# First transforms from half-height matrices into a two-bank buffer, fewer banks for the other tiles, and tap 0 added on GpSimd

## The chip, the cores and the metric

The kernel runs on one core of one Trainium2 chip. The metric is the device time of one execution in microseconds (us), as the median of several runs. TensorE (PE in the profile) multiplies matrices into PSUM, which has eight banks of 128 x 512 floats; VectorE (DVE) and ScalarE (ACT) read PSUM and SBUF; GpSimd (POOL) works on SBUF alone; SyncE (SP) issues most DMAs. All data are float32.

## The reference, cut to what matters

Four layers in a row update x (2048 positions, 512 channels): A, B, A, B. Each layer is a long causal convolution per channel.

```python
def A(q, k, v, shift_k, ssm_k, ssm_D):
    k_shift = sum of 4 shifted copies of k, each times shift_k     # short causal convolution
    kv = k_shift * v
    y  = irfft(rfft(kv, 4096) * rfft(ssm_k, 4096))[:2048]          # per channel
    return q * (y + kv * ssm_D)

def B(u, ...):
    K[d, l] = 2 * Re(sum over 128 modes n of C[d, n] * exp(A[d, n] * dt[d] * l))
    y = irfft(rfft(u, 4096) * rfft(K, 4096))[:2048]                # per channel
    return y + u * D_skip

x = q
x = x + A(layernorm(x), k, v, ...)
x = x + B(layernorm(x), ...)
x = x + A(layernorm(x), k, v, ...)      # same k, v: the same convolution result as in the first A
x = x + B(layernorm(x), ...)            # same K
```

`ssm_D` and `D_skip` are direct terms: the same as adding them to element 0 (tap 0) of the convolution kernels before the transform.

## The kernel before, in words

**The transform.** An FFT of 4096 points is done as two matrix stages with a transpose between them. The sequence is laid out on 128 partitions as two halves of 64 rows (a = 0, 1), 16 positions deep, and the channels are taken in 4 quarters (q) of 4 groups (g) of 32. The first stage (`fwd_rows`, L171, tile `pf`) multiplies each group by the matrix `wz[:, a, :]`, in which only the 64 rows of half a hold numbers and the other 64 hold zeros: a matmul over all 128 rows, two per step, with a step of 16 channels, so that both halves of a step fill one bank. VectorE then transposes 32 x 32 blocks from `pf` into `z` (L195, or L193 where a step is 32 channels wide). Where the tag `f1` exists, which is only in the second half of the program, a step is 32 channels: two matmuls of 512 columns over 64 rows each, with the matrix `w1`, stand side by side on the upper and the lower rows of the array and write two banks. The second stage (`f2_chunk`, L200, tile `pu`) does 8 chunks of 4 matmuls for a quarter.

**Spectra.** `spectrum_quarter` makes the spectrum of a convolution kernel: it loads a group `kk` by DMA (from the input `ssmk_in` for A, from `kdram` for B), transforms it with `fwd_group`, and adds the direct term with a third matmul of one row and 16 columns per step (L187, from `dr`, "tap 0"). After the eight chunks, ScalarE copies each `pu` to `pc` (L245) and a DMA writes it to `spec`.

**The convolution.** `convolution` takes for each of 32 steps a chunk `pu` of the data's spectrum, reads it with ScalarE (`sw`, L277, L278) and VectorE (`vv`, L279), multiplies by the loaded spectrum `kab` on GpSimd (L281, L282), transforms back in two stages (`pi` L291, `po` L312) and hands groups to `finish`.

**Two streams at once.** `diagonal` computes A: the four spectra of A, the short convolution and product (`gated`, L604 to L619, stored to `kv_d`), and the convolution of A. `stream` computes the kernel K of B (`taps`): `mags` (matmul L467 into `pm`, exponential on ScalarE, L469), `angles` (L479, L483, L484, tile `pa`), `waves` (sines on ScalarE, L492 to L494), `products` (L505 to L509 on GpSimd and VectorE) and `contract` (L520, tile `pk`), for 16 groups of 4 pieces; exponentials are made for two groups at a time, twelve in a run, because sines and exponentials need different tables on ScalarE. After every four groups it makes one quarter of B's spectrum. `run_steps` takes one step of `stream` and two of `diagonal` in turn; a list scheduler then fixes the order on each engine, which is in-order on the chip.

**PSUM in this first half.** Three banks with the tag `c1` hold `pf`, `pu`, `pi` and `po` of A and the first forward transforms of B's data; two banks `pm` hold the exponents and also `pf` and `pu` of B's spectrum; two hold `pa`, one holds `pk`. In the second half the banks are divided anew (four `c1`, two buffers of two banks `f1`).

**Afterwards.** `gated_update` loads the result of A (`yaq` from `ya_d`), updates x and its statistics (L715 to L724), then `conv_b(0)` convolves with K, a second `gated_update` uses the same A, and `conv_b(1)` writes the output. The first quarter of `conv_b(0)`'s forward transforms (`steps_b`, q = 0) is placed before the banks are divided anew.

Of the kernel before, what the change touches and what calls it, by code (L numbers as in the profile page):

```python
# [9 lines left out]
F32 = mybir.dt.float32  # L10
# [89 lines left out]
def kernel(ctx: ExitStack, tc: tile.TileContext, out, x_in, kv_in, ssmk_in, ssmd_in,  # L100
                           la_in, ai_in, cr_in, ci_in, ldt_in, ldtb_in, dsk_in,
                           w1_in, w2_in, mm_in, w4_in, minus_in, tt_in, tg1_in, tg2_in, dbg=None):
    nc = tc.nc
    V, S, G, T = nc.vector, nc.scalar, nc.gpsimd, nc.tensor
# [30 lines left out]
    wz = cpool.tile([128, 2, 128], F32, name="wz")  # L135
# [7 lines left out]
    psum, w1, swapped = {}, [], [None]  # L143

    def bank(name, tag="c1"):
        pool, bufs = psum[tag]
# [13 lines left out]
    def fwd_rows(src, pf, j, step, rows, full):  # L160
        for a in (1, 0):
            half = slice(0, 128) if full else slice(64 * a, 64 * a + 64)
            w = wz[:, a, :] if full else w1[0][half, :]
            rhs = src(half, j, step)[:, rows, :]
            o = pf[:, a].rearrange("p x t r -> p t x r")[:, rows]
            if len(rhs.shape) == 4:
                o = o.rearrange("p t (i x) r -> p t i x r", i=rhs.shape[2])
                rhs = rhs.rearrange("p t i (x r) -> p t i x r", r=2)
            else:
                rhs = rhs.rearrange("p t (x r) -> p t x r", r=2)  # L170
            yield T.matmul(o, w, rhs, start=True, stop=True)  # L171

    def fwd_group(src, z, c0, n, step, tap0=None, first=None, tag="c1", full=True, early=None):
        for j in range(0, n, step):
            rest = slice(0, 16)
            if early is not None:
                pf, rest = early, slice(8, 16)
            elif step == 32:
                pf = wide_bank()
            else:  # L180
                both = bank("pf", tag).rearrange("p (x n r) -> p x r n", n=32, r=2)
                pf = both.rearrange("p x r (a t) -> p a x t r", a=2)
            for i in fwd_rows(src, pf, j, step, rest, full):
                if first is not None:
                    after(i, first)
            if tap0 is not None:
                T.matmul(pf[:, 0, :, 0, :], wz[0:1, 0, :],  # L187
                         tap0[:, j:j + step].rearrange("p (x r) -> p x r", r=2), start=False, stop=True,
                         skip_group_check=True)
            zr = z[:, (c0 + j) // 2:(c0 + j + step) // 2].rearrange("p x k r -> p x r k")  # L190
            if step == 32:
                for r in range(2):
                    V.transpose(zr[:, :, r], pf[..., r].rearrange("p a x t -> p x a t"))  # L193
            else:
                V.transpose(zr, both)  # L195
# [28 lines left out]
    def spectrum_quarter(which, q, src, pool, zlast, zb, tag):  # L224
        z = pool.tile([128, 64, 32, 2], F32, name="zk", tag="z", bufs=zb)
        dr = pool.tile([1, 128], F32, name="dr", tag="dr", bufs=1)
        nc.sync.dma_start(dr, (ssmd_in, dsk_in)[which][:, 128 * q:128 * q + 128])
        for g in range(4):
            kk = pool.tile([128, 512], F32, name="kk", tag="kk", bufs=3 - which)
            nc.sync.dma_start(kk, src[4 * q + g])  # L230
            if which == 0:
                kv = kk.rearrange("p (t c) -> p t c", c=32)
                view = lambda ps_, j, n: kv[ps_, :, j:j + n]
            else:
                kv = kk.rearrange("p (i t c) -> p t i c", i=4, c=8)
                view = lambda ps_, j, n: kv[ps_, :, j // 8:(j + n) // 8, :]
            fwd_group(view, z, 32 * g, 32, 16, dr[:, 32 * g:32 * g + 32],
                      zlast[-zb] if len(zlast) >= zb else None, tag)
            yield
        for c in range(NCH):  # L240
            pu, ins = f2_chunk(z, c, None, tag)
# [182 lines left out]
    pctx = ExitStack()  # L424
    pp = pctx.enter_context(tc.tile_pool(name="ps", bufs=1, space=PSUM, reuse_waits="tile"))
    NPA = 2
    NPM = 2
    psum["c1"] = (pp, 7 - NPA - NPM)
    psum["pm"] = (pp, NPM)

    for tag, bufs in (("c1", 7 - NPA - NPM), ("pa", NPA), ("pk", 1)):
        pp.tile([128, 512], F32, name=tag, tag=tag, bufs=bufs)
    wk = sbuf(gctx, "wk")
    kp = sbuf(gctx, "spec_k")
    NT = 3
# [154 lines left out]
    with ExitStack() as actx:  # L590
# [42 lines left out]
        def steps_a(q):  # L633
# [7 lines left out]
            def fwd(g):  # L641
                if g == 0:
                    z[0] = ap.tile([128, 64, 32, 2], F32, name="zu", tag="z", bufs=ZA)
                u = us[g]
                fwd_group(lambda ps_, j, n: u[ps_, :, j:j + n], z[0], 32 * g, 32, 16, None, zlast[4 + q - ZA])
                if g < 3:
                    load(g + 1)
            turns = [lambda g=g: fwd(g) for g in range(4)]
# [46 lines left out]
    nc.sync.dma_start(w1[0], w1_in)  # L695
# [67 lines left out]
    def steps_b(rnd, q):  # L763
# [152 lines left out]
```

## Time and profile before

| what | value |
|---|---|
| median of the three runs | 803.81 us (801.69 to 804.71) |
| the profiled execution's own time | 802.01 us |
| its span, from the first to the last instruction | 800.2 us |
| mean granted TensorE clock | 0.862 |
| PE, DVE, ACT, POOL busy | 676.5, 604.8, 479.2, 531.9 us |

An engine's busy time is the sum of its instructions' spans; the ends of matmuls are modelled. One row for a float32 matmul stands twice in the profile's counts, since the chip runs it as two passes. PEclk is the share of the full TensorE clock that was granted. A DMA's time to landing runs from its issue.

### The profile page before, as it was taken

The numbers are of one execution on the slowest core, as the hardware profiler recorded it, in microseconds if no ns is written. First come the engines' busy times: TensorE is split into PE (matmuls) and PEld (weight loads), VectorE is DVE, ScalarE is ACT, GpSimd is POOL, SyncE is SP. The second block draws the span as 40 slices with busy tenths as digits, with TensorE's granted clock in tenths as the row PEclk, the third lists the DMA queues.
The fourth block names the chain that finished last, engine by engine and source line by source line (L and its number), as shares of the span: only waits on it lengthen the run. The fifth ranks groups of instructions, "written<-read, shape, count | busy, mean of one in ns | idle before, by whom it ended". The sixth has DMA issues, their size and how long they took to land.

```text
span 800.2 us, 14659 instructions
## 1 busy us (share of the span) xinstructions
PE 676.5 (85%) x5192; PEld 475.6 (59%) x5192; DVE 604.8 (76%) x939; ACT 479.2 (60%) x881; POOL 531.9 (66%) x464
## 2 busy tenths in 40 slices
PE   3779988999989999999899867889789840898996
PEld 2555755667667766757666444666557720476673
DVE  7767856989996958756849699625568989878775
ACT  4144443535478884785884687628746625878572
POOL 4966744967868975777964678206666836288783
PEclk9686765869999999999999755699989975999998
DMA  9586254557378463664541891238968541078792
GB/s 329 195 263 249 94 174 151 187 171 253 130 222 231 131 184 97 192 187 153 125 119 54 268 313 42 76 115 206 238 169 197 147 106 53 1 182 220 200 247 99
DMA packets 89614, 135.49 MB, mean 169 GB/s; under 512 B 8509, under 2 KB 37701, under 8 KB 89029
## 3 DMA queue, kind: packets, MB, share of 16 engines
q1 hardware_dynamic: 88644, 132.13, 56.8%
q0 software_dynamic: 896, 2.43, 1.0%
q8 instruction: 41, 0.67, 0.4%
q14 instruction: 33, 0.26, 0.1%
HBM read 98.87 MB, written 35.65 MB: 168 GB/s over the span
## 4 chain that ended last, share of the span: by engine, by line
PE 27%; DVE 14%; ACT 4%; DMA 4%; issue 3%; POOL 2%; SPq 1%; DVEq 0%; POOLq 0%; ACTq 0%
PE pu L200 8%; PE pf L171 6%; PE pi L291 5%; PE po L312 5%; DVE x L722 3%; DVE ut L715 2%; DMA kab<-spec 2%; POOL sw L281 1%; DMA yaq<-ya_d 1%; DVE w L306 1%; PE pk L520 1%; DVE vv L279 1%; POOL vv L282 1%; DVE tt L506 1%; DVE st L822 1%
## 5 line engine op out<-in xcount | busy, mean ns | idle before, releaser
L281 POOL TENSOR_TENSOR sw<-sw,kab 128x512 f32<-128x512 f32 x96 | 125.4, 1313 | 76.5 <-ACT sw L278 65.5
L505 POOL TENSOR_TENSOR xy<-tt,m 128x512 f32<-128x512 f32 x64 | 89.7, 1402 | 62.7 <-ACT tt L494 54.6
L200 PEld LDWEIGHTS pu<-zu,w 128*128 128x128 f32 x768 | 94.6, 191 | 51.1 <-DVE vv L279 18.4
L200 PE MATMUL pu<-zu,w 128*128 128x128 f32 x768 | 108.4, 283 | 12.2 <-DVE vv L279 11.8
L171 PE MATMUL pf<-kk,wz 128*128 128x256 f32 x256 | 96.2, 512 | 24.7 <-DMA kk<-ssmk_in 15.9
L279 DVE TENSOR_TENSOR vv<-pu,kab 128x512 f32<-128x512 f32 x96 | 64.7, 679 | 64.6 <-ACT sw L278 32.0
L282 POOL TENSOR_TENSOR vv<-vv,sw 128x512 f32<-128x512 f32 x76 | 100.1, 1320 | 14.8 <-DVE vv L279 12.0
L291 PE MATMUL pi<-vv,mm 128*128 128x128 f32 x768 | 106.9, 284 | 3.4 <-DVE vv L279 2.8
L291 PEld LDWEIGHTS pi<-vv,mm 128*128 128x128 f32 x768 | 95.3, 195 | 15.9 <-issue 9.4
L277 ACT ACTIVATE sw<-pu 64x512 f32<-64x512 f32 x96 | 57.1, 595 | 63.0 <-PE pu L200 52.1
L200 PE MATMUL pu<-zk,w 128*128 128x128 f32 x512 | 80.4, 313 | 5.5 <-DVE zk L195 3.6
L492 ACT ACTIVATE tt<-pa 128x512 f32<-128x512 f32 x64 | 38.5, 601 | 75.4 <-PE pa L484 64.1
L200 PEld LDWEIGHTS pu<-zk,w 128*128 128x128 f32 x512 | 74.8, 223 | 14.4 <-DVE zk L195 4.1
L171 PEld LDWEIGHTS pf<-kk,wz 128*128 128x128 f32 x256 | 57.8, 247 | 42.8 <-issue 16.0
L245 ACT COPY pc<-pu 128x512 f32<-128x512 f32 x64 | 37.5, 592 | 63.1 <-PE pu L200 45.7
L469 ACT ACTIVATE m<-pm 128x512 f32<-128x512 f32 x96 | 54.2, 598 | 31.5 <-PE pm L467 30.6
L506 DVE TENSOR_TENSOR tt<-tt,m 128x512 f32<-128x512 f32 x64 | 71.6, 1118 | 0.4
L507 DVE SCALAR_TENSOR_TENSOR xy<-tt,m 128x256 f32<-128x256 f32 x64 | 51.1, 798 | 24.0 <-ACT tt L493 20.2
L195 DVE STREAM_TRANSPOSE zk<-pf 128x512 f32<-128x512 f32 x64 | 44.5, 703 | 28.0 <-PE pf L187 27.8
L312 PE MATMUL po<-w,w 128*64 128x512 f32 x192 | 56.1, 671 | 7.8 <-DVE w L306 6.7
L509 POOL TENSOR_TENSOR xy<-tt,m 128x256 f32<-128x256 f32 x64 | 60.9, 951 | 0.0
L520 PE MATMUL pk<-xy,tt 128*32 128x64 f32 x2048 | 53.7, 244 | 5.8 <-POOL xy L509 3.1
(141 smaller groups left out, 1310.3 us busy)
## 6 DMA issues: line engine op xcount, KB each, us to landing
kab<-spec SPq DMA_DIRECT2D x188, 256.0 KB, 4.0
spec<-pc SPq DMA_DIRECT2D x64, 256.0 KB, 2.4
kvt<-kv_in SPq DMA_DIRECT2D x16, 624.0 KB, 6.5
yaq<-ya_d SPq DMA_DIRECT2D x8, 1024.0 KB, 5.5
kk<-ssmk_in SPq DMA_DIRECT2D x16, 256.0 KB, 5.1
kv_d<-u SPq DMA_DIRECT2D x16, 256.0 KB
kdram<-ks SPq DMA_DIRECT2D x64, 64.0 KB, 2.4
kk<-kdram SPq DMA_DIRECT2D x16, 256.0 KB, 2.6
```

The lines of the kernel that those rows point to most:

```text
L171: yield T.matmul(o, w, rhs, start=True, stop=True)
L200: ins = T.matmul(pu[:, i, :], w2[:, c * CK + i, :], z[:, :, c * CK + i, :], start=True, stop=True)
L277: S.mul(sw[0:64], pu[64:128], -1.0)
L279: V.tensor_mul(vv, pu, kabs[s][:, 0])
L281: (V if last else G).tensor_mul(sw, sw, kabs[s][:, 1])
L282: (V if last or s % add_dve == add_dve - 1 else G).tensor_add(vv, vv, sw)
L291: i1s[t] = T.matmul(pi[:, i, :], mm[:, c * CK + i, :], vvs[t][:, i, :], start=True, stop=True)
L312: ins = T.matmul(po[64 * a:64 * a + 64], w4, ws[g][:, :, 16 * a:16 * a + 16, :].rearrange("p x t r -> p t x r"), start=True, stop=True, ti ...
L505: G.tensor_mul(xy[:, :, :, 32:64], tt[:, :, :, 1:33], m1[:, :, 32:64][:, None].to_broadcast([128, 2, 8, 32]))
L506: (G if (4 * gi + k) % E2P == E2P - 1 else V).tensor_mul(e2, e2, m2[:, None].to_broadcast([128, 2, 8, 32]))
L509: (V if (4 * gi + k) % XLP == XLP - 1 else G).tensor_mul(xy[:, 0, :, 0:32], tt[:, 0, :, 0:32], m1[:, :, 0:32])
L520: T.matmul(pk[32 * i4:32 * i4 + 32, 2 * k + i, :], e2[:, r, 4 * i + i4, :], xy[:, r, 4 * i + i4, :], start=r == 0, stop=r == 1, tile_posit ...
```

## The change

What it does:

- All first transforms but those of the first group of `conv_b(1)` use a step of 32 channels with `wz[half, a, :]`, 64 rows each, into a buffer of two banks; the separate matrix `w1` and its DMA go.
- In the first half of the program, PSUM is divided anew: `c1` two banks (three before), `pm` one (two before), `f1` one buffer of two banks (new), `pa` two and `pk` one as before. All `pf` of the first half are now in `f1`; `pu` of B's spectrum stays in `pm`.
- Tap 0 is no longer a matmul. GpSimd adds `dr` to row 0 of the loaded `kk` (1 x 32 elements) before the group's transform.

```diff
     def fwd_rows(src, pf, j, step, rows, full):
         for a in (1, 0):
             half = slice(0, 128) if full else slice(64 * a, 64 * a + 64)
-            w = wz[:, a, :] if full else w1[0][half, :]
+            w = wz[half, a, :]
...
-    def fwd_group(src, z, c0, n, step, tap0=None, first=None, tag="c1", full=True, early=None):
+    def fwd_group(src, z, c0, n, step, first=None, tag="c1", full=False, early=None):
...
-            if tap0 is not None:
-                T.matmul(pf[:, 0, :, 0, :], wz[0:1, 0, :],
-                         tap0[:, j:j + step].rearrange("p (x r) -> p x r", r=2), start=False, stop=True,
-                         skip_group_check=True)
...
     # spectrum_quarter
+            d = dr[:, 32 * g:32 * g + 32]
...
-            fwd_group(view, z, 32 * g, 32, 16, dr[:, 32 * g:32 * g + 32],
-                      zlast[-zb] if len(zlast) >= zb else None, tag)
+                d = d.rearrange("p (i c) -> p i c", c=8)
+
+            G.tensor_add(kv[0:1, 0], kv[0:1, 0], d)
+            fwd_group(view, z, 32 * g, 32, 32, zlast[-zb] if len(zlast) >= zb else None, tag)
...
-    NPM = 2
-    psum["c1"] = (pp, 7 - NPA - NPM)
+    NPM = 1
+    psum["c1"] = (pp, 2)
     psum["pm"] = (pp, NPM)
+    psum["f1"] = (pp, 1)
...
     # steps_a
-                fwd_group(lambda ps_, j, n: u[ps_, :, j:j + n], z[0], 32 * g, 32, 16, None, zlast[4 + q - ZA])
+                fwd_group(lambda ps_, j, n: u[ps_, :, j:j + n], z[0], 32 * g, 32, 32, zlast[4 + q - ZA], full=False)
...
-    w1.append(xp.tile([128, 128], F32, name="w1"))
-    nc.sync.dma_start(w1[0], w1_in)
...
     # steps_b
-                fwd_group(src(c), z[0], 16 * c, 32, 32 if "f1" in psum else 16,
-                          full="f1" not in psum or q == 0 and c < 2 * EF, early=early.get(c))
+                fwd_group(src(c), z[0], 16 * c, 32, 32, full=rnd == 1 and q == 0 and c < 2 * EF,
+                          early=early.get(c))
```

More of the change, by code (lines that the diff above doesn't have):

```diff
@@ L141 @@
     var, rs, nm, nb = [cpool.tile([128, 16], F32, name=n) for n in ("var", "rs", "nm", "nb")]
-    psum, w1, swapped = {}, [], [None]
+    psum, swapped = {}, [None]
     def bank(name, tag="c1"):
@@ L426 @@
     NPA = 2
-    NPM = 2
-    psum["c1"] = (pp, 7 - NPA - NPM)
+    NPM = 1
+    psum["c1"] = (pp, 2)
     psum["pm"] = (pp, NPM)
-    for tag, bufs in (("c1", 7 - NPA - NPM), ("pa", NPA), ("pk", 1)):
-        pp.tile([128, 512], F32, name=tag, tag=tag, bufs=bufs)
+    psum["f1"] = (pp, 1)
+    for tag, bufs, shape in (("c1", 2, [128, 512]), ("f1", 1, [128, 2, 512]), ("pa", NPA, [128, 512]), ("pk", 1, [128, 512])):
+        pp.tile(shape, F32, name=tag, tag=tag, bufs=bufs)
     wk = sbuf(gctx, "wk")
```

## The prediction

> **What bounds the kernel now.** I read the busy table of the page first, then the busy time by stretches, then the groups of instructions, then the waits, and last the chain that ended last where no engine is full.
>
> ```profile
> span 800.2 us, 14659 instructions
> 60.00:140.00 80.00, 73.09 (x453) 48.39 (x454) 54.41 (x77) 33.64 (x57) 46.64 (x37) 0.61 0.50 167
> 140.00:240.00 100.00, 91.93 (x866) 66.29 (x864) 93.48 (x136) 51.63 (x91) 78.97 (x64) 0.87 0.60 192
> 240.00:380.00 140.00, 136.62 (x1288) 100.83 (x1288) 98.71 (x139) 104.16 (x181) 105.87 (x95) 0.99 0.60 168
> 380.00:440.00 60.00, 55.39 (x547) 37.14 (x547) 44.58 (x57) 42.80 (x75) 40.09 (x34) 1.00 0.36 100
> 440.00:500.00 60.00, 43.28 (x400) 28.64 (x399) 53.56 (x85) 46.17 (x92) 45.09 (x34) 0.64 0.68 208
> 500.00:540.00 40.00, 33.46 (x246) 26.24 (x245) 17.85 (x40) 18.07 (x39) 5.05 (x10) 0.81 0.31 94
> ACT tt L492 <- PE pa L484: 60.6, 25, 8.9
> ACT m L469 <- PE pm L467: 28.9, 16, 5.6
> ```
>
> The stretches give, after their length, the busy time of PE, of its weight loads, of DVE, ACT and POOL, then the granted clock and the DMA load. The change touches only what lies before 540. From 60 to 440 PE is busy 357.0 of 380 us: 91% from 60 to 140, at a clock of 0.61, and 98% from 240 to 380 at 0.99. The last two rows (the waits of that stretch: total, times, longest) say the same from the other side: ScalarE sits behind PE. Only from 140 to 240 is another engine as full (DVE, 93.5 of 100). From 440 to 500 DVE has most, with the update of x; from 500 to 540 nothing is full, and a chain of dependent steps sets the time.
>
> **What the change takes from PE.** Here are the groups of instructions (busy us, mean ns), then the first transforms alone (PE's busy time and count by stretch) and tap 0 alone, then pieces of PE's timeline (start, length).
>
> ```profile
> L171 PE MATMUL pf<-kk,wz 128*128 128x256 f32 x256 | 96.2, 512 | 24.7 <-DMA kk<-ssmk_in 15.9 <-DVE zk L195 5.5 <-DMA kk<-kdram 2.1
> L195 DVE STREAM_TRANSPOSE zk<-pf 128x512 f32<-128x512 f32 x64 | 44.5, 703 | 28.0 <-PE pf L187 27.8
> L193 DVE STREAM_TRANSPOSE zu<-pf 128x512 f32<-128x512 f32 x56 | 35.8, 686 | 13.7 <-PE pf L171 13.5
> L467 PE MATMUL pm<-tg,rw 64*128 64x512 f32 x96 | 46.6, 556 | 13.6 <-ACT m L469 8.9 <-DVE rw L460 4.8
> L469 ACT ACTIVATE m<-pm 128x512 f32<-128x512 f32 x96 | 54.2, 598 | 31.5 <-PE pm L467 30.6
> L245 ACT COPY pc<-pu 128x512 f32<-128x512 f32 x64 | 37.5, 592 | 63.1 <-PE pu L200 45.7 <-DMA spec<-pc 17.2
> L263 POOL COPY kab<-kab 1x128 f32<-1x128 f32 x12 | 4.7, 392 | 4.0 <-DMA kab<-spec 3.5
> ```
> ```profile
> 60.00:140.00 80.00, 28.22 (x60) 15.97 (x60) 0.61 0.50 167
> 140.00:240.00 100.00, 30.81 (x96) 20.25 (x96) 0.87 0.60 192
> 240.00:380.00 140.00, 33.16 (x124) 21.59 (x124) 0.99 0.60 168
> 380.00:440.00 60.00, 9.97 (x36) 6.18 (x36) 1.00 0.36 100
> ```
> ```profile
> 60.00:140.00 80.00, 8.64 (x30) 7.05 (x30) 0.61 0.50 167
> 140.00:240.00 100.00, 7.10 (x32) 5.50 (x32) 0.87 0.60 192
> 240.00:380.00 140.00, 3.12 (x16) 2.34 (x16) 0.99 0.60 168
> 380.00:440.00 60.00, 3.12 (x16) 2.34 (x16) 1.00 0.36 100
> ```
> ```profile
> 21.85 1.13 PE L171 MATMUL pf<-kk,wz 128*128 128x256 f32 x4
> 22.91 0.39 PE L187 MATMUL pf<-dr,wz 1*128 1x16 f32 x2
> 23.23 1.13 PE L171 MATMUL pf<-kk,wz 128*128 128x256 f32 x4
> ...
> 602.24 1.13 PE L171 MATMUL pf<-u,w 64*128 64x512 f32 x4
> 603.30 1.16 PE L200 MATMUL pu<-zu,w 128*128 128x128 f32 x8
> ```
>
> A step of 16 channels stands as four records and takes 1.06 us at full clock (21.85 to 22.91); tap 0 behind it takes 0.32 (to 23.23). A group of 32 channels is two steps, so 2.12 us, and 2.76 with tap 0. The new form is in the trace already, in the second half: the two matmuls of a group over half the rows run side by side and take 1.06 us (602.24 to 603.30) for all 32 channels.
>
> By stretch: 60 records are 7.5 groups. From 60 to 140 the old form holds PE for 28.2 + 8.6 = 36.9 us; the new one 7.5 x 1.06 / 0.61 = 13.0, so 24 us go. From 140 to 240 (12 groups): 37.9 less 12 x 1.06 / 0.87 = 14.6, so 23. From 240 to 380 (15.5 groups): 36.3 less 16.4, so 20. From 380 to 440 (4.5 groups): 13.1 less 4.8, so 8. Together 75 of PE's 357 us.
>
> **What of that can become time.** PE would hold 49, 69, 117 and 47 us of 80, 100, 140 and 60, and another engine decides. From 60 to 140 that is DVE with 54.4; from 140 to 240 DVE with 93.5, so nothing is to be had there; from 240 to 380 POOL with 105.9 and ACT with 104.2; from 380 to 440 DVE with 44.6. None of them gets to work without gaps. I let the fullest be busy 85% of the time (an estimate between the 68 to 76% that they hold now in three of the stretches and the 93% of DVE in the fourth): 64, 100, 125 and 52 us, which saves 16, 0, 15 and 8, or 39 us. That is the upper end. The lower end is nothing, if the missing banks give it all back. I take half, 20 us, for this reason: three banks of `c1` become two, but the `pf` that used them leave, so `pu`, `pi`, `po` lose little; `pm` loses much more.
>
> **What the lost bank of `pm` costs.** Now PE fills one bank while ScalarE reads the other, and twelve exponentials in a run can follow each other at 0.60 us (L469). With one bank each waits for its matmul: 0.60 + 0.56 (L467) is 1.16 us, at least. That is 0.56 x 96 = 54 us more of latency over 8 runs. Where PE and ScalarE have other work between, and from 60 to 440 both have, it is hidden: the order that the scheduler built puts `pu`, `pi` or `pf` between most of these matmuls. One run has no such cover, that of the last two groups of taps, behind the end of A; it is 12 x 0.56 = 7 us longer. It lies where DVE is full with the update of x, and I count nothing for it, 7 at most. The chunks of B's spectrum have the same single bank, and there the last quarter counts, next.
>
> **GpSimd's adds.** 32 adds of one row: the nearest row is the copy of one row, 0.39 us (L263), so 12.5 us over a POOL that is busy 271.6 of 380; nothing at best, where POOL is idle. Each add waits for its `kk` at the head of POOL's queue, and products and steps of `gated` stand behind it; PE waited 15.9 us for `kk` from the input, 13 of them before its first matmul, and 2.1 for `kk` from `kdram` (row of L171), so the loads come early enough elsewhere and I count nothing before the last quarter. DVE's transposes stay as many, and as long: two per group of 0.69 (L193, reading two banks with a stride) against 0.70 (L195). The buffer `f1` is single, so the next group's matmuls wait for both: a group takes 1.06 + 1.37 = 2.4 us at least, against 2.76 on PE before; other matmuls fit in between.
>
> **From 440 on.** No engine's relief counts here but what lies on the chain that ended last:
>
> ```profile
> 445.86 0.54 SPq L695
> ...
> 499.18 1.71 PE pf L171 x4
> ...
> 501.43 2.00 PE pf L171 x4
> ...
> 505.83 2.01 PE pf L171 x4
> ...
> 508.27 1.06 PE pf L171 x4
> ...
> 519.93 2.57 DMA kk<-kdram
> ...
> 528.17 3.64 PE pu L200 x32
> 532.47 2.07 PE pu L200 x16
> 535.18 2.95 PE pu L200 x24
> ```
>
> The issue of the load of `w1` (0.54) goes. The four steps at 499 to 509, 6.8 us, become two groups of about 1.06 / 0.64 = 1.7, that is 3.3, but the second waits for the first's transposes (1.4): 2 us are saved. Then the last quarter of B's spectrum: its last `kk` lands at 522.5; the add puts 0.4 us before the transform, and at most 1.3 if POOL has a product before it. The eight chunks run from 528.17 to 537.1 (the last row holds 16 of their records and 8 of `conv_b(0)`, so 535.18 + 2/3 of 2.95): 9 us, with two banks. With one bank each chunk is matmuls (3.64 / 4 = 0.91), copy (0.59) and two hand-overs of about 0.2 (estimate): 1.9, so 15 us, 6 more. The four groups of `conv_b(0)` now fit between chunks, where PE waits anyway; without that cover they would cost 4 x 1.06. Sum of this part: -0.5 - 2 + 0.4 + 6 = +4 us; bounds -2 (chunks limited by their DMAs as now) and +13 (with the 7 and 1.3).
>
> **The sum.** 802.0 (the profiled execution) - 20 + 4 = 786. The median of the runs shown is 1.8 us above that execution, so 788 against 803.8.
>
> **The rivals.** (1) The banks do not matter: then all 39 us come, and the end takes its lower bound: 802 - 39 - 2 = 761, 763 beside the median. For it: PE waits little for banks now (8.9 us for `m` in the row of L467). Against it: ScalarE's table order and POOL's products come in bursts.
>
> (2) Slower: the one bank of `pm` becomes the pace of the taps. Place: the eight runs of exponentials, behind which no sine may start, and the 32 chunks of B's spectrum, each 0.6 us longer or more. Price: 54 + 32 x 0.7 = 76 us if none is hidden. It decides from the point where more than 20 of these 76 lie on the path besides the 6 that I count; with half of it there, 38, the time is 802 - 20 - 2 + 38 = 818, or 820 beside the median; with 32, 814. For it: already 28.9 us of ScalarE's waits are for `pm` with two banks. Against it: only one run in eight stands without other work around it.
>
> (3) The clock falls. PE has the clock of 0.99 only where it is busy 98%; at 91% (60 to 140) it has 0.61. If from 240 to 440, busy 192.0, less 28, it fell to the 0.81 of 500 to 540, PE would need 164 / 0.81 = 202 of those 200 us: 2 us more than now. With half of the 16 from 60 to 140, and the end as forecast, that is 802 + 2 - 8 + 4 = 800, or 802 beside the median; at 0.61 the 164 would be 269, far slower. The Trainium skill has such a rule in "TensorE: Matmul & The Clock Gate", Part 1, on a second failure mode: where a kernel cycles through PSUM banks and TensorE is idle for moments between groups of matmuls, the clock gate swings between half and full. By it, fewer banks would lower the clock. This trace bears it out only in part: 0.61 stands in a stretch in which PE was 91% busy.
>
> (4) The change does not do what it says: DVE, slowed by POOL beside it, bounds all of 60 to 440, and the 75 us of PE turn into idle time: 802 + 4, 808 beside the median.
>
> **How the numbers follow.** Chances: forecast 0.47 (own range 778 to 798), rival 1 0.16, rival 2 0.22, rival 3 0.07, rival 4 0.08. The likeliest is 788. The range goes from rival 1 at 763 to rival 2 with 32 of its us on the path, 814, about the middle of rival 2, so 0.11 to 0.15 stay outside. About 0.5%, 4 us, is what a measurement of this kernel can tell from no change. Faster by more than that (below 799.8): nearly all of the forecast (0.45) and rival 1 (0.16), so 0.61. Within it: 0.02 of the forecast, 0.04 of rival 3, 0.04 of rival 4: 0.10. Slower: rival 2 (0.22), 0.03 of rival 3 and 0.04 of rival 4: 0.29.
>
> **What the profile after would show.** Right: the groups `pf<-kk` with 64x512 and half the records, about 1.06 us start to start at full clock; no L187; PE's share from 240 to the end of A well under 98%, with DVE, ACT and POOL denser; the end of A (the loads of `yaq`) 15 to 25 us earlier; the last chunks of `pc` 1.9 us apart. Rival 2 would show `pm` waiting for `m`, and ScalarE's waits for `pm` far over 28.9 us; rival 3 a PEclk well under 1 from 240 to 440; rival 4 PE idle and the end of A where it is now. The forecast is wrong if the end of A does not move, or if the stretch from there to the second half grows by over 13 us.

## The result and the profile after

The changed kernel takes 849.97 us (median of four runs, 847.71 to 853.22) beside 802.75 us for the kernel before on the same chip: a ratio of 1.0635, 95% interval 1.0559 to 1.071. The profiled execution took 847.71 us, its span is 845.6. The change is slower by 6%, where 788 us were forecast. Some executions of a kernel are over 1.5% slower than its fastest; the ratios, here and below, leave these out and can differ a little from the quotients of the medians, which are of all.

The page's head and the same stretches as before come first: after the stretch's length, the busy time of PE, of its weight loads, of DVE, ACT and POOL, then the granted clock and the DMA load.

```profile
span 845.6 us, 14085 instructions
60.00:140.00 80.00, 62.13 (x482) 41.43 (x481) 69.00 (x88) 36.14 (x63) 65.90 (x56) 0.78 0.70 231
140.00:240.00 100.00, 69.52 (x592) 41.20 (x595) 71.00 (x110) 43.77 (x74) 54.74 (x51) 0.64 0.47 149
240.00:380.00 140.00, 113.93 (x1128) 75.29 (x1120) 94.81 (x128) 95.55 (x163) 97.11 (x89) 0.90 0.49 136
380.00:440.00 60.00, 53.76 (x465) 33.93 (x464) 45.04 (x55) 39.84 (x68) 39.78 (x37) 0.90 0.50 142
440.00:500.00 60.00, 48.98 (x453) 28.19 (x452) 36.19 (x48) 38.94 (x67) 32.37 (x29) 0.78 0.46 141
500.00:540.00 40.00, 23.19 (x183) 13.75 (x183) 37.77 (x67) 33.80 (x72) 26.76 (x20) 0.58 0.46 145
```

From 60 to 440 PE is busy 299.3 us, not 357.0, and no engine takes its place: over the same 380 us DVE went from 291.2 to 279.9, ACT from 232.2 to 215.3, POOL from 271.6 to 257.5. From 60 to 140 DVE and POOL do more than before (A's product `gated` runs ahead), from 140 to 240 far less, and there PE fell from 92 to 70 us. Over the 380 us all four have more idle time.

The first transforms and the exponents, as groups (busy us, mean ns, idle before):

```profile
L171 PE MATMUL pf<-kk,wz 64*128 64x512 f32 x128 | 62.4, 878 | 57.3 <-issue 20.0 <-DMA kk<-ssmk_in 13.6 <-DMA kk<-kdram 12.1
L236 POOL TENSOR_TENSOR kk<-kk,dr 1x32 f32<-1x32 f32 x32 | 14.1, 441 | 38.2 <-DMA kk<-kdram 33.1 <-DMA kk<-ssmk_in 5.0
L469 ACT ACTIVATE m<-pm 128x512 f32<-128x512 f32 x96 | 57.5, 599 | 62.8 <-PE pm L467 59.7
L467 PE MATMUL pm<-tg,rw 64*128 64x512 f32 x96 | 65.8, 685 | 25.8 <-ACT m L469 25.7
```

The new form and the adds are there, and no tap 0 on PE. But ScalarE now waits 59.7 us for the matmuls of the exponents (30.6 before), and PE 25.7 us for the exponentials (8.9 before). A stretch of ScalarE's timeline (start, length, idle before and what ended it), then of PE's, shows both halves of that:

```profile
133.85 0.60 ACT L469 ACTIVATE m<-pm 128x512 f32<-128x512 f32 x1 [1.14 <-PE pm L467]
135.32 0.60 ACT L469 ACTIVATE m<-pm 128x512 f32<-128x512 f32 x1 [0.88 <-PE pm L467]
136.81 0.60 ACT L469 ACTIVATE m<-pm 128x512 f32<-128x512 f32 x1 [0.88 <-PE pm L467]
...
147.64 0.60 ACT L469 ACTIVATE m<-pm 128x512 f32<-128x512 f32 x1 [5.52 <-PE pm L467]
149.12 0.60 ACT L469 ACTIVATE m<-pm 128x512 f32<-128x512 f32 x1 [0.88 <-PE pm L467]
155.59 0.60 ACT L469 ACTIVATE m<-pm 128x512 f32<-128x512 f32 x1 [5.88 <-PE pm L467]
```
```profile
145.14 2.08 PE L171 MATMUL pf<-kk,wz 64*128 64x512 f32 x4 [3.65 <-DVE zk L189]
146.19 1.41 PE L467 MATMUL pm<-tg,rw 64*128 64x512 f32 x1
148.29 0.79 PE L467 MATMUL pm<-tg,rw 64*128 64x512 f32 x1 [0.69 <-ACT m L469]
153.08 2.08 PE L171 MATMUL pf<-kk,wz 64*128 64x512 f32 x4 [4.00 <-issue]
154.14 1.41 PE L467 MATMUL pm<-tg,rw 64*128 64x512 f32 x1
```

Where nothing stands between, an exponential follows the last after 1.48 us: matmul, hand-over, exponential, hand-over, in turn. Where something does, it is worse. The exponential at 147.64 waited 5.52 us, because its matmul (146.19) stands in PE's queue behind the first transform at 145.14, and that one waited 3.65 us for the transposes that free the single buffer `f1`. At 155.59 it is the same, behind the transform at 153.08; that one starts as the last transposes (to 152.98) and GpSimd's add for it (to 153.09) end. With a second bank such a matmul could have been placed ahead of the transform.

**Which stream ends last.** These rows are the end of A (its last copy `ya`), the end of the taps (the last product `ks`) and the first read of `conv_b(0)`'s chunks (`sw`, the start of the second half), first of the kernel before, then of the changed one:

```profile
442.87 0.59 ACT L656 COPY ya<-po 128x512 f32<-128x512 f32 x1 [0.49 <-PE po L312]
513.41 0.64 DVE L530 TENSOR_TENSOR ks<-pk,dt 128x256 f32<-128x256 f32 x1
539.07 0.59 ACT L277 ACTIVATE sw<-pu 64x512 f32<-64x512 f32 x1
```
```profile
481.90 0.59 ACT L656 COPY ya<-po 128x512 f32<-128x512 f32 x1 [0.20 <-PE po L311]
557.11 0.62 DVE L530 TENSOR_TENSOR ks<-pk,dt 128x256 f32<-128x256 f32 x1
588.11 0.59 ACT L276 ACTIVATE sw<-pu 64x512 f32<-64x512 f32 x1
```

The taps end 43.7 us later, the second half starts 49.0 us later (5.3 more, in the last quarter of B's spectrum), and from there to the end the changed kernel takes 3.6 us less (257.5 of its span against 261.1). That is the whole difference of the spans, 45.4. A also ends 39 us later, but it is the taps that count, as the experiments show. Counted from the start of the first to the start of the last of each run of twelve, the eight runs of exponentials took 145 us before and 234 after: 89 more. The rest of the taps, between the runs, took 46 less.

### The profile page after: what moved, and what is told of

Read it like the earlier page. It is cut to its first block, busy times and chain, and to the rows that moved or that the text cites. A ratio compares the mean times of both kernels' runs of the same rounds, so it can differ in the third digit from the quotient of the medians.

```text
span 845.6 us, 14085 instructions
## 1 busy us (share of the span) xinstructions
PE 627.9 (74%) x4856; PEld 402.0 (48%) x4856; DVE 618.5 (73%) x939; ACT 486.2 (57%) x883; POOL 536.6 (63%) x496
## 4 chain that ended last, share of the span: by engine, by line
PE 31%; DVE 15%; ACT 11%; DMA 6%; issue 6%; POOL 4%; SPq 1%; DVEq 0%; POOLq 0%; ACTq 0%
PE pu L196 10%; PE pi L290 6%; PE po L311 5%; PE pf L171 4%; DMA kab<-spec 3%; DVE x L720 3%; POOL sw L280 2%; PE pm L467 2%; PE pk L520 2%; DVE ut L713 2%; PE pa L484 1%; DVE tt L506 1%; ACT u L772 1%; DVE vv L278 1%; ACT tt L494 1%
## 5 line engine op out<-in xcount | busy, mean ns | idle before, releaser
L505 POOL TENSOR_TENSOR xy<-tt,m 128x512 f32<-128x512 f32 x64 | 92.1, 1438 | 64.8 <-ACT tt L494 38.7
L196 PE MATMUL pu<-zu,w 128*128 128x128 f32 x768 | 112.1, 289 | 13.4 <-DVE vv L278 9.8
L281 POOL TENSOR_TENSOR vv<-vv,sw 128x512 f32<-128x512 f32 x76 | 99.2, 1306 | 17.9 <-DVE vv L278 14.6
L171 PE MATMUL pf<-kk,wz 64*128 64x512 f32 x128 | 62.4, 878 | 57.3 <-issue 20.0
L196 PE MATMUL pu<-zk,w 128*128 128x128 f32 x512 | 88.9, 327 | 20.3 <-ACT pc L244 7.1
L196 PEld LDWEIGHTS pu<-zk,w 128*128 128x128 f32 x512 | 79.5, 233 | 44.8 <-ACT pc L244 13.4
L469 ACT ACTIVATE m<-pm 128x512 f32<-128x512 f32 x96 | 57.5, 599 | 62.8 <-PE pm L467 59.7
L467 PE MATMUL pm<-tg,rw 64*128 64x512 f32 x96 | 65.8, 685 | 25.8 <-ACT m L469 25.7
L189 DVE STREAM_TRANSPOSE zu<-pf 128x512 f32<-128x512 f32 x96 | 62.0, 688 | 23.3 <-PE pf L171 15.6
L506 DVE TENSOR_TENSOR tt<-tt,m 128x512 f32<-128x512 f32 x64 | 68.6, 1072 | 4.0 <-ACT tt L494 3.8
L507 DVE SCALAR_TENSOR_TENSOR xy<-tt,m 128x256 f32<-128x256 f32 x64 | 57.0, 892 | 18.8 <-ACT tt L493 13.0
L171 PE MATMUL pf<-u,wz 64*128 64x512 f32 (+2 forms) x200 | 61.8, 647 | 4.4 <-DVE zu L189 3.1
```

Of the source, the lines that this page charges most:

```text
L196: ins = T.matmul(pu[:, i, :], w2[:, c * CK + i, :], z[:, :, c * CK + i, :], start=True, stop=True)
L281: (V if last or s % add_dve == add_dve - 1 else G).tensor_add(vv, vv, sw)
L467: mt = T.matmul(pm, rows[gi][hs, 1, :], rhs, start=True, stop=True)
L505: G.tensor_mul(xy[:, :, :, 32:64], tt[:, :, :, 1:33], m1[:, :, 32:64][:, None].to_broadcast([128, 2, 8, 32]))
L506: (G if (4 * gi + k) % E2P == E2P - 1 else V).tensor_mul(e2, e2, m2[:, None].to_broadcast([128, 2, 8, 32]))
```

## The experiments

Each was timed beside the kernel before on the same chip (797 to 803 us there); ratios are to it, with their 95% intervals.

### The parts of the change, alone

The changed kernel with tap 0 back on TensorE:

```diff
-            G.tensor_add(kv[0:1, 0], kv[0:1, 0], d)
+            # in fwd_group, behind fwd_rows
+            T.matmul(pf[:, 0, :, 0, :], wz[0:1, 0, :], tap0[...], start=False, stop=True, ...)
```

> The changed kernel with tap 0 back on TensorE as a one-row matmul behind each group; half-height matrices and the new banks stay. Theory Q (GpSimd's adds stop TensorE: each add stands in GpSimd's queue behind the short convolution's products or behind a DMA, the transform waits for the add, and the exponents' matmuls wait behind the transform): most of the 47 us come back, 805 to 820 us. Theory B (one bank for pm paces the exponentials, whatever does tap 0): little comes back, 838 to 852 us.

870.3 us, ratio 1.098 (1.0857 to 1.1102). Neither range was met, but the time moved away from Q's: GpSimd's adds are not the cause. Within the change they bring some 20 us by the medians (28 by the ratios; this kernel and the changed one were not timed beside each other).

The kernel before with the new division of the banks for `pm` and `c1`, and two banks empty:

```diff
-    NPM = 2                     # c1: 7 - NPA - NPM = 3
+    NPM = 1                     # c1: 2
```

> The kernel before with two banks c1 and one pm and two banks left empty; full-height matrices and tap 0 on TensorE as before. Theory B: at least as slow as the change, 845 us or more, since the transforms keep their full cost on TensorE and lose their banks as well. Theory Q: near the kernel before, 800 to 820 us.

898.49 us, ratio 1.1305 (1.1184 to 1.1426), as theory B said: the new division of the banks alone costs more than the whole change.

The kernel before with only tap 0 moved to GpSimd (one-bank steps as before):

```diff
+            G.tensor_add(kv[0:1, 0], kv[0:1, 0], d)
-            fwd_group(view, z, 32 * g, 32, 16, dr[...], ...)
+            fwd_group(view, z, 32 * g, 32, 16, None, ...)
```

> The kernel before with tap 0 added by GpSimd and nothing else changed. Theory Q: most of the loss shows here too, 825 to 845 us. Theory B: near the kernel before, or a little faster since 64 small matmuls (20 us of TensorE) go, 790 to 808 us.

801.57 us, ratio 1.0059 (1.0016 to 1.0103). PE loses all of tap 0, 22 us of its busy time from 60 to 440 (331.2 there, 357.0 before), and no bank is lost; the time does not fall. A ends at 446.0, the taps at 510.8, and the second half starts at 538.6, all within 3.2 us of before. There is a new wait, that of the transforms for the adds, which wait for late loads:

```profile
PE pf L171 <- POOL kk L240: 31.4, 6, 12.6
POOL kk L240 <- DMA kk<-kdram: 17.0, 4, 12.4
```

It does not explain where the 22 us went: 24.8 of the 31.4 lie before 60, where PE waits for the same loads in the kernel before (15.9), and only 1.5 between 60 and 440. Nor does this run show that PE at 98% is no bound, since only 3.1 of the 22 us lie in the stretch from 240 to 380.

The kernel before with one bank of `pm`, the second left empty, all else unchanged:

```diff
-    NPM = 2
+    NPM = 1                     # c1 stays 3
```

> The kernel before with one bank for pm instead of two, three for c1, one bank left empty. Theory B: 830 us or more. Theory Q: 800 to 812 us. If this is slow and the run with both bank cuts is slower still, c1's lost bank costs the difference.

896.84 us, ratio 1.1252 (1.1106 to 1.1398). The bank of `pm` alone costs about 97 us; the bank of `c1` adds 2 (898.49). So the rest of the change (the half-height form and tap 0) gives some 48 back. The three marks of this kernel, and its waits (total, times, longest):

```profile
420.57 0.58 ACT L656 COPY ya<-po 128x512 f32<-128x512 f32 x1 [1.36 <-PE po L312]
595.72 0.64 DVE L530 TENSOR_TENSOR ks<-pk,dt 128x256 f32<-128x256 f32 x1
635.52 0.59 ACT L277 ACTIVATE sw<-pu 64x512 f32<-64x512 f32 x1
```
```profile
ACT m L469 <- PE pm L467: 70.2, 63, 4.7
PE pm L467 <- ACT m L469: 36.9, 39, 4.7
```

A ends 22 us *earlier* than before, and the kernel is 97 us slower: A's end does not set the time here, the taps' end does (82.3 later; the last quarter of B's spectrum, with one bank, adds 14.1). The eight runs of exponentials took 213 us, 68 more than before; the two engines' waits for each other grew by 40 and 28, together as much.

Turn by turn (from one exponential of a run to the next, in the two traces), the loss is the same with other work between and without. Where PE starts no other matmul between the two of the exponents, the mean turn went from 0.78 us (35 turns) to 1.58 (36); where it does, from 2.22 (53 turns) to 2.99 (52). And the last run, which has no other matmul in any of its turns in this kernel, took 16.0 us; before, with other work in two of its turns, it took 15.1. Nearly all of the 68 lies in the seven runs that have other work around them.

### Is it the exponents, or B's spectrum in the same bank?

The changed kernel with B's spectrum chunks in `c1`, so that `pm` holds exponents alone; then the same on the kernel before, with one bank of `pm` and four of `c1`:

```diff
-    todo.append(spectrum_quarter(1, m // 16, kdram, kp, zlast_k, 1, "pm"))
+    todo.append(spectrum_quarter(1, m // 16, kdram, kp, zlast_k, 1, "c1"))
```

> The changed kernel with the chunks pu of B's spectrum in c1 (two banks) instead of pm; the one bank pm is left to the exponents. Theory R (the round trip of matmul and exponential through one bank costs the time): 835 to 850 us, as in the change. Theory S (the one bank ties two chains together: exponents and spectrum chunks take it in program order, so the next exponents wait for a chunk that waits for its own loads, transposes and copies): most of the loss goes, 790 to 815 us, and what TensorE saves can begin to show.

> The kernel before with the same eight banks divided otherwise: one pm for the exponents alone, four c1 that also take all first transforms and chunks of B's spectrum. Theory R: 860 us or more, as with one pm for both (897). Theory S: 795 to 815 us, near the kernel before.

856.61 us, ratio 1.0716 (1.0645 to 1.0787), and 904.33 us, 1.1281 (1.1205 to 1.1357). The first lies a little above R's range and far above S's. The second uses all eight banks and is as slow as with one bank empty: the number of banks is not it.

The kernel before with its two banks of `pm` split, one for the exponents and one for B's spectrum:

```diff
-    NPM = 2
+    NPM = 1                     # exponents
...
-    psum["pm"] = (pp, NPM)
+    psum["ps"] = (pp, 1)        # pf and pu of B's spectrum
```

> The kernel before with its two pm banks split: one bank for the exponents, one for B's spectrum (first transforms and chunks). Theory R: the exponents have one bank, 860 us or more. Theory S: the two chains no longer wait for each other, 790 to 815 us.

889.36 us, ratio 1.1112 (1.1023 to 1.1201). It is the exponents' single buffer (theory R), not their sharing with B's spectrum (S). With B's spectrum in a bank of its own, this costs 87 us.

The changed kernel with two banks of `pm` and one of `pa`:

```diff
-    NPA = 2
-    NPM = 1
+    NPA = 1
+    NPM = 2
```

> The changed kernel with pm back at two banks, paid for with one bank of pa (one instead of two). Theory R and theory S both give back what pm cost, 800 to 815 us, if pa's lost bank costs little; if pa's bank is worth as much, since the angles' matmuls and VectorE's rounding take turns in it, 840 us or more.

891.7 us, ratio 1.113 (1.1054 to 1.1207). The runs of exponentials are short again (127 us), and the rest of the taps takes 427 us instead of 274: a single `pa` is worse than a single `pm`.

### Half buffers, and the half-height form alone

The exponents as two of 256 columns, in the two halves of one bank (before, then the changed kernel), and in two banks (before):

```diff
+    pmx = pp.tile([128, 2, 256], F32, name="pm", tag="pm", bufs=1)    # or [128, 2, 512]
+        for e in range(2):
+            pm = pmx[:, e]                                            # or pmx[:, e, 0:256]
+            T.matmul(pm, rows[gi][hs, 1, :], rhs[:, nr * e:nr * e + nr, :], start=True, stop=True)
+            i = S.activation(m[:, 256 * e:256 * e + 256], pm, AF.Exp)
```

> The kernel before with one bank for the exponents (as in the run of that layout at 904.33 us: c1 four banks, B's spectrum in c1), but the bank is used as two halves of 256 columns: each exponential becomes two of 128x256, and TensorE may fill one half while ScalarE reads the other. Theory R (the round trip: with a single buffer matmul and exponential take turns, 1.2 to 1.5 us per 512 columns; a bank as such is not what is missing): with two half buffers the pace is ScalarE's, two of about 0.41 us (estimate between the 128x128 at 0.31 and the 128x512 at 0.60), 0.81 instead of 0.60 with two banks, so about a third of the loss stays: 832 us, 810 to 850. Rival O (the loss comes from the order that the scheduler makes when the taps have one bank, A's work running ahead of the taps, or from ScalarE and TensorE meeting in one bank): it stays as it was, 885 to 915.

> As the first of these kernels, but the two halves of an exponent lie in two different banks (c1 three banks, as in the kernel before; B's spectrum in c1). Theory R: within 12 us of the first kernel, since both have two buffers of 256 columns. Rival C (TensorE and ScalarE hamper each other in one bank): over 15 us faster than the first. Rival O: near the kernel before, 800 to 820, where the first stays near 900.

> The changed kernel with B's spectrum chunks in c1 (856.61 us in its own run) and the one bank of the exponents used as two halves of 256 columns. Theory R: the bursts of exponentials shorten from about 240 us in sum to about 150 to 180, and the time falls to 800 to 830 us. Rival O: 848 to 866, bursts as before.

988.44 us, ratio 1.2393 (1.2155 to 1.2632); 979.07 us, 1.2282 (1.2164 to 1.2399); 962.81 us, 1.2075 (1.1955 to 1.2194). All three expectations missed: as the trace of the second shows, the halves of one tile were not used as two buffers. Here it is, with the halves in two banks, on PE and then on ScalarE:

```profile
160.69 0.38 PE L472 MATMUL pm<-tg,rw 64*128 64x256 f32 x1 [0.47 <-ACT m L473]
161.55 0.38 PE L472 MATMUL pm<-tg,rw 64*128 64x256 f32 x1 [0.47 <-ACT m L473]
```
```profile
161.11 0.38 ACT L473 ACTIVATE m<-pm 128x256 f32<-128x256 f32 x1 [0.47 <-PE pm L472]
161.97 0.38 ACT L473 ACTIVATE m<-pm 128x256 f32<-128x256 f32 x1 [0.47 <-PE pm L472]
```

Each matmul still waits for the exponential just before it, though that one reads the other bank: a turn of 0.86 us is 0.38 + 0.38 and two hand-overs of about 0.05. So these are kernels with 192 turns instead of 96, each turn shorter, and the two made from the kernel before lose 177 and 186 us, where 96 turns lose 87 to 102.

The changed kernel with the full-height matrices, two matmuls of 512 columns one after the other into the same two banks:

```diff
-    fwd_group(..., 32 * g, 32, 32, ..., tag)
+    fwd_group(..., 32 * g, 32, 32, ..., tag, full=True)     # all first transforms of the first half
```

> The changed kernel with the same banks and the same two-bank buffer f1, but the first transforms of the first half from the matrices of full height (128 rows, two matmuls of 512 columns one after the other, 2.12 us for a group instead of 1.06 at full clock). It gives back TensorE's relief alone. Theory H (the halves are worth what the layout's loss of about 95 us was lowered by, less the 20 that tap 0 on GpSimd is worth): 850 + 28 = 878 us, 868 to 892. Rival W (TensorE waits for ScalarE so much in the changed kernel that its relief is worth little): 846 to 858.

864.04 us, ratio 1.084 (1.0732 to 1.0949), against 1.0635 for the change: the half-height form is worth about 14 us within the change, between what theories H (18 to 42) and W (at most 8) said. With the 20 of tap 0 that is 34 of the 48 that the rest of the change gives back; the other 14 (the transforms' own buffer `f1` is left) were not measured alone. These are differences of kernels that were not timed beside each other, good to some 10 us by the intervals.

### What in the turns costs?

The kernel before with the halved exponents in its two independent tiles; and with its two banks as one tile, filled by two matmuls and read by one exponential of 1024 columns:

```diff
+            pm = pp.tile([128, 512], F32, name="pm", tag="pm", bufs=NPM)[:, 0:256]    # first kernel, twice per exponent
...
+        pair.append(pp.tile([128, 2, 512], F32, name="pm", tag="pm", bufs=1))         # second kernel
+        i = S.activation(m, pm, AF.Exp)                                               # m: 128 x 2 x 512
```

> The kernel before (same banks) with each exponential made as two of 128x256, in turn in the two independent tiles of pm: 192 exponentials as in the two runs with half tiles (988.44 and 979.07 us), but no strict turn: the next matmul need not wait for the exponential just before. Theory T (what costs is the number of strict turns between TensorE and ScalarE, each about 1 us: 97 to 102 us for 96 turns, 177 to 186 for 192): only ScalarE's extra work stays, (2 x 0.38 - 0.60) x 96 = 15 us at most: 802 to 825 us. Rival N (the greater number of small instructions and hand-overs costs, whatever the buffers): 940 to 990.

> The kernel before with the two banks of pm as one tile: two matmuls of 512 columns fill it, then one exponential of 1024 columns reads it. B's spectrum goes through c1 (three banks as before). 48 strict turns instead of 96. Theory T: about 48 us lost, 802 + 48 = 850, 835 to 865. Rival L (the length of the turns in sum costs: 48 x (2 x 0.56 + 1.1 + 0.1) = 111 us, against 96 x 1.26 = 121 with one bank): as with one bank, 885 to 910.

860.78 us, ratio 1.0723 (1.0633 to 1.0814), and 824.34 us, 1.0277 (1.0198 to 1.0356). Neither theory holds. The first should have cost 15 us and cost 58; the second should have cost 48 (by number) or 83 to 108 (by length) and cost 22, and there A ends at 484.1, 41 us later than before, and the taps at 505.4, 8 earlier. Their exponentials as groups (the profiled execution of the first took 868.97 us):

```profile
L471 ACT ACTIVATE m<-pm 128x256 f32<-128x256 f32 x192 | 65.6, 384 | 55.0 <-PE pm L470 53.6 <-DMA raw<-rows_d 0.7
L476 ACT ACTIVATE m<-pm 128x1024 f32<-128x1024 f32 x48 | 49.3, 1026 | 46.7 <-PE pm L471 46.0
```

ScalarE waits more in both than before (30.6): 61 times in the first and 20 times in the second, where it was 18.

The changed kernel with one set of three banks for A, B's spectrum and the exponents; and with two of `pm`, which A's `pi` shares, and one of `c1`:

```diff
-        pm = pp.tile([128, 512], F32, name="pm", tag="pm", bufs=NPM)
+        pm = bank("pm")                                     # first kernel: c1 of three banks
...
-                pi = bank("pi")
+                pi = bank("pi", "pm" if which == 0 else "c1")    # second kernel: pm 2, c1 1
```

> The changed kernel with the bank of pm given to c1: three banks serve A's tiles, B's spectrum and the exponents by turns. Theory T: no tile has a single buffer but f1, so the exponents cost what they did before: 785 to 820 us. Rival M (mixed in one set of banks, an exponent waits for A's readers and A for ScalarE's exponentials): 850 or more.

> The changed kernel with two banks of pm (exponents, B's chunks and A's pi) and one of c1 (A's pu and po). Theory T: the 96 strict turns of the exponents go, 32 of pu and 16 of po come: 850 - 97 + 48 = about 801, 785 to 830. Rival M: the single bank of c1 holds up A and the time stays at 845 or more.

851.63 us, ratio 1.0609 (1.0527 to 1.0691), and 873.25 us, 1.09 (1.0831 to 1.0969). Rival M holds in both. In the first the runs of exponentials take 94 us, fewer than before, and the rest of the taps 417 instead of 274. The wait has moved, not gone: the products wait for the sines, 71.3 us here and 38.7 in the changed kernel.

```profile
POOL xy L505 <- ACT tt L494: 71.3, 7, 20.0
```

What holds the sines up was not followed. The wait of 17.9 us for GpSimd's add, which the expectation for the set of five below names, delays nothing: it ends at 45.7 us, with the first exponential, which starts at 48.2 in the kernel before.

### A third bank, and one set of five

The kernel before with three banks of `pm` and two of `c1`; and with all five in one set:

```diff
-    NPM = 2
+    NPM = 3                     # c1: 2
...
-        pm = pp.tile([128, 512], F32, name="pm", tag="pm", bufs=NPM)
+        pm = bank("pm")         # second kernel: c1 of five banks, B's spectrum in c1 too
```

> The kernel before with three banks of pm and two of c1. Theory V (what a bank of the exponents is worth is the waiting of ScalarE and TensorE for each other that it takes away; with two banks 30.6 + 8.9 us of it are left): with a third bank up to half of these go, less about 2 us for the bank of c1: 785 to 802. Rival D (two buffers are all that alternating needs; the rest of the waiting is for TensorE's other work): 801 to 812.

> The kernel before with its three banks of c1 and two of pm as one set of five that A's tiles, B's spectrum and the exponents take by turns. Theory V: no tile has fewer banks than before on the whole, 785 to 810. Rival M (mixed in one set, an exponent waits for A's readers, as in the changed kernel with the three banks of c1 and pm in one set, where one wait for GpSimd's add behind a late load cost ScalarE 17.9 us): 820 or more.

840.59 us, ratio 1.0536 (1.0433 to 1.0639), and 841.02 us, 1.0574 (1.0481 to 1.0667). For the first both theories missed; for the second M holds. The marks of the first:

```profile
518.61 0.58 ACT L656 COPY ya<-po 128x512 f32<-128x512 f32 x1 [2.82 <-PE po L312]
460.69 0.65 DVE L530 TENSOR_TENSOR ks<-pk,dt 128x256 f32<-128x256 f32 x1
577.48 0.59 ACT L277 ACTIVATE sw<-pu 64x512 f32<-64x512 f32 x1 [6.08 <-PE pu L200]
```

With a third bank for the exponents and one less for `c1`, the taps end 52.7 us earlier than before, and A 75.7 us later: now A sets the time, and the second half starts 58.9 us behind it. Whether A is late for its lost bank of `c1` or for the other order was not separated.

With one, two and three banks of `pm` in the kernel before, the runs of exponentials took 213, 145 and 96 us, and the taps ended at 595.7, 513.4 and 460.7. Short runs alone do not make the taps early, though: in the set of five the runs took 64 us, and the taps still ended at 547.9, 34 later than before. No kernel was found that beats the one before.

**What the marks say together.** In 18 of the 20 profiles the second half starts 26 to 40 us behind the last tap, whatever A does (A's end there lies 91 to 215 us before it). The two others are the three-bank kernel, in which A sets the time, and the one with pairs. In that one A's end, 89.6 us before the second half, does not explain it; its last spectrum chunk (563.6, 58 us behind its last tap) comes, in the chain that ended last, after a load of `kk` from 530.0 to 537.6 and three stores of `spec` up to 562.9, and why these are late was not followed. From the start of the second half to the end it is 255 to 265 us in all 20.

## Why the prediction was wrong

**The step that failed** is "What the lost bank of `pm` costs": 54 us of latency, of which "Where PE and ScalarE have other work between, and from 60 to 440 both have, it is hidden", and "I count nothing for it". With nothing else changed, that bank costs 97 us (87 to 102 in the two runs in which B's spectrum has other banks). None of the 54 is hidden: the runs of exponentials are 68 us longer, a turn loses 0.8 us whether PE has other work between or not, and the one run that was to be 7 us longer for want of cover lost 0.9. The work between is no cover but part of the delay: a matmul of the exponents that can only start after the last exponential stands in PE's queue behind whatever PE took up meanwhile (5.52 us at 147.64). And what stands behind the exponentials is the stream that ends last.

**The mark was wrong as well.** The prediction measured success by PE's fullness from 60 to 440 and by the end of A. In the kernel before, A ended 96.2 us before the second half started, and the three-bank kernel shows that 58.9 are enough: A had some 37 us to spare (an estimate from these two kernels), the taps none. The rows were there: in the chain quoted, the last quarter of B's spectrum follows the taps, 70 us after A's end. PE's relief without a lost bank bought nothing either: taking tap 0's 22 us from it changed the time by +0.6%. Whether PE was the bound in the stretch at 98% no run settles.

Step by step:

- PE's relief: PE's busy time in first transforms and tap 0 from 60 to 440 was 124.1 us (the prediction's rows added up); of the changed kernel's tile `pf` alone, the four stretches give

```profile
sum 380.00, PE 57.09; mean PE 14.27
```

  so 67 us went, where 75 were forecast, and a part of that is work moved out of the stretch (37 groups instead of 39.5). Right in kind, somewhat less in size.
- What of it becomes time: half of 39, or 20, was forecast; within the change the half-height form gives about 14 and tap 0 about 20, together 34; in the kernel before tap 0's part is nothing. That is more than forecast, and the step behind the forecast (which engine is next) has no support, since from 60 to 440 no engine became fuller.
- GpSimd's adds: 0.441 us each against 0.39, "nothing" in sum; they are a gain within the change. Right enough; in the kernel before they are neutral (801.57).
- "`pu`, `pi`, `po` lose little" by the third bank of `c1`: with one `pm`, giving it up as well moves A's end from 420.6 to 473.4, and the time by 2 us. Little only because A has time to spare; in the three-bank kernel, which also has two banks of `c1`, A ends 75.7 us later and sets the time.
- From 440 on, +4 was forecast, with the eight chunks 1.9 us apart (6 us more than before). Measured from the last tap to the second half: +5.3, and chunks of `pc` start at these times:

```profile
572.39 0.59 ACT L244 COPY pc<-pu 128x512 f32<-128x512 f32 x1 [2.17 <-PE pu L196]
575.08 0.59 ACT L244 COPY pc<-pu 128x512 f32<-128x512 f32 x1 [2.10 <-PE pu L196]
...
580.34 0.59 ACT L244 COPY pc<-pu 128x512 f32<-128x512 f32 x1 [2.04 <-PE pu L196]
582.22 0.59 ACT L244 COPY pc<-pu 128x512 f32<-128x512 f32 x1 [1.29 <-PE pu L196]
584.09 0.59 ACT L244 COPY pc<-pu 128x512 f32<-128x512 f32 x1 [1.29 <-PE pu L196]
585.97 0.59 ACT L244 COPY pc<-pu 128x512 f32<-128x512 f32 x1 [1.29 <-PE pu L196]
```

  The last four are 1.88 us apart. The first five are 2.6 to 2.8 apart: the four transforms of `conv_b(0)` between them, which were to fit in "where PE waits anyway", add some 0.8 us each, the same mistake as with the exponents. So the eight chunks took 7.0 us more than before from the first to the last copy, the way from the last tap to the first copy 3.2 less, and that from the last copy to the second half 1.5 more. The 1.9 itself came out by luck: the hand-overs are 0.08 and 0.05 here, not 0.2, and the matmuls of a chunk take 1.16 us, not 0.91. The bound of +13 adds up to 12. Such a sum of matmul, copy and hand-overs for one buffer was used here for eight chunks and counted as time; for the 96 exponents it was made without the hand-overs and counted as hidden.

**The rivals.** Rival 2 named the mechanism, the place and the sign that would show it (ScalarE's waits for `pm` far over 28.9 us; over the span they went from 30.6 to 59.7). Its price, 76 us with half of it on the path, was too small: the bank alone costs 97. Its argument against itself, that only one run in eight stands without other work around it, is the failed step again. Rival 1 is out. Rival 3, the clock: it fell from 0.87 to 0.64 between 140 and 240, where PE went from 92 to 70 us busy, and from 0.99 to 0.90 between 240 and 380. The rule of the Trainium skill that the prediction named ("TensorE: Matmul & The Clock Gate", Part 1, second failure mode) agrees in direction there, but not from 60 to 140, where PE is less busy (62 us, 73 before) at a higher clock (0.78, 0.61 before). The rival's premise, a clock of 0.99 only where PE is busy 98%, was misread: in the prediction's own rows the clock is 1.00 from 380 to 440, where PE is busy 92%. The clock alone does not explain the loss: with full-height matrices the mean clock is 0.861, as in the kernel before (0.862), and the time is 864.04 us. Rival 4 is out: DVE and POOL are less busy than before from 60 to 440.

A price that the Trainium skill states beforehand stands in "TensorEngine Tiling (Array Packing)", under Gotcha 1: row tiles that run side by side must write different banks. The two banks of `f1` are that price. By these runs the form that needs them returns 14 us, and the bank that was taken for it from the exponents costs 97 in the kernel before.

**What stays open.** How the loss of one bank comes to 97 us is shown in its parts (the runs of exponentials +68, the taps between them +16, the last spectrum quarter +14, the second half -1, the start of the taps -1; 95.4 between the spans), not derived. It goes neither with the number of turns (48: 22 us; 96: 87 to 102; 192: 177 to 186, but 58 with two tiles) nor with their length. The untested rival is the order: each division of the banks also gives the scheduler another one, which shifts time between A and the taps (three banks: -53 and +76); how much of each loss is order and how much waiting was not separated. Nor was a version tried that hands A's 37 us to the taps.

## What to carry to other kernels

Before pricing the relief of the busiest engine, find which of two interleaved streams ends last and how much the other has to spare; here TensorE's relief brought less than a lost buffer cost, and the end of the wrong stream was watched. The second buffer between two in-order engines was worth more here than the round trip it hides (87 to 102 us against 54), and other work in the two queues did not hide its loss. A buffer can be priced alone, by taking the bank away from the kernel before and leaving it empty, before anything is built that needs it (the price then includes what the other order does).

## What was not expected of the hardware

ScalarE's exponential takes 0.384 us for 256 columns, 0.599 for 512 and 1.026 for 1024 (means of the groups above; 0.599 is the changed kernel's): doubling the width costs 0.215 and then 0.427, so some 0.17 us of each is independent of it. Two engines that take turns on one buffer need about 0.05 us for each hand-over (0.86 us for 0.38 + 0.38, at a granted clock of 1.00 from 160 to 162 us of the run with halves in two banks). An add of one row of 32 elements on GpSimd takes 0.441 us on average, 0.24 at the shortest.
